# The first batch's values of an agent-attention kernel, loaded as 112 and 8 rows in place of 128

## The chip, the cores and the metric

One core of one Trainium2 chip runs the whole program. The metric is the device time of one execution, in microseconds; the kernel before is given by the median of three runs.

## What is computed

Two layers follow each other. The attention has 49 agents per batch between queries and keys (B = 2 batches, N = 12480 tokens, C = 128 channels), the second layer is a leaky-ReLU MLP of width 2048 without biases:

```
a2k     = softmax(scale * agents @ k^T)      # 49 x N, per batch
agent_v = a2k @ v                            # 49 x C, per batch
q2a     = softmax(scale * q @ agents^T)      # N x 49
x       = q2a @ agent_v                      # N x C
h       = x @ w_in;  g = max(0.01 * h, h);  out = g @ w_out
```

## The kernel before

The host lays the values out as `v[b, p, j, c]`, 120 rows `p` of 104 columns `j` of 130 floats (128 channels, a one for the denominator, a zero). A chunk `c` is eight columns, so that a row of a chunk is 8 * 130 * 4 = 4160 contiguous bytes, and a batch has 13 chunks. Keys are laid out as `k[b, :, j, :]` with 128 channels as rows of 8 * 120 * 4 = 3840 bytes, again 13 chunks.

The work has two stages. In the first, some 53 us long, the first batch's attention is done while everything it needs is streamed in: the 13 chunks of keys, the weights as eight transfers of 512 KB (64-bit words, taken apart by `conv_bits`, line 262, and its companions), two blocks of queries, then the 13 chunks of values. All loads are issued by SyncE (SP) in the order of the string `ORDER` (line 134): `"kwqwkkkqwkkkwkkkkkkwvvwvvvvvvvvvwvvwq"`. In the second stage a loop over 52 blocks of 480 tokens runs `mm1`, `relu_hi`, `relu_lo` and `mm2` in eight steps a block, with the queries' chain, and in the first 26 blocks the second batch's attention, put into its side steps.

The order of the first stage's instructions on each engine is worked out at build time by `Plan` (line 19) from costs written by hand: each load is a step on "sp" and one on "dma", each consumer a step on its engine. A values' chunk is a step of 1280 on "dma" (line 1124). The order is then fixed; on the chip an engine waits where its operand isn't there yet. `heat` (line 1106) are products of zeros that the plan puts into TensorE's gaps.

`load_v` (line 217) loads one chunk of values into a tile of a ring of nine (`ld`, shared with the keys). For the first batch it transfers 128 rows, of which the last eight are the first rows of the second batch, and nobody reads them. For the second batch it transfers the 120 rows alone (line 224). SP issues each transfer when its tile is free and when an earlier transfer's completion counter is free again.

The consumer in the first stage is `k_av32` (line 561): for each column a product of the exponentials of the scores, `s_sb`, with `v_t[b, c][:TP, j, :]`, rows 0 to 119, sixteen matmul records per chunk (each fp32 product shows as two), 208 in all, summed in one PSUM tile `av`. The chunks are taken in the order in which they are loaded. When the last is in, the chain `f_copy` (574), `f_tr`, `f_den`, `f_rec`, `f_avT`, `m_half` (666), `m_hi_of`, `m_lo_of` ends in the first `mm1` (869).

For the last two transfers of weights, `conv_bits` (273, 274) waits on VectorE for the weights to land; `conv_low` (289), `conv_sign` (296) and `conv_mul` (303) come behind it. `ww_tr` (316) and `ww_mm` (330) are products of the weights on TensorE. `p_move` and `p_dup` (856, 860) are SP's transfers from SBUF to SBUF of 64 and 32 rows.

Of the kernel before, what the change touches and what calls it, by code (L numbers as in the profile page):

```python
# [74 lines left out]
def tile_agent_attention_then_leaky_mlp(  # L75
# [27 lines left out]
    nc = tc.nc  # L103
# [3 lines left out]
    P = 128  # L107
    TP = 120
# [108 lines left out]
    def load_v(b, c):  # L217

        t = ld.tile([P, CH, C + 2], F32, tag="ld", name="vt")
        j = slice(c * CH, (c + 1) * CH)  # L220
        if b == 0:
            nc.sync.dma_start(out=t, in_=v.rearrange("b p j c -> (b p) j c")[:P, j, :])
        else:
            nc.sync.dma_start(out=t[:TP], in_=v[b, :, j, :])
        v_t[b, c] = t
# [811 lines left out]
    for b in range(1, B):  # L1037
# [21 lines left out]
        for h in range(NH):  # L1059
            s = n0 + h * NP // 2  # L1060
            if h % 2 == 0:
                c = h // 2
                at(s - 5, load_v, b, c)
                at(s, k_sub, b, c, nc.gpsimd)
                at(s + 2, k_exp, b, c)
            at(s + 3, k_ehi, b, h, h, nc.scalar)
            at(s + 3, k_elo, b, h, h, nc.gpsimd)
            at(s + 1, k_vhi, b, h, h, nc.vector)
            at(s + 2, k_vlo, b, h, h, nc.gpsimd)
            if h % 2:  # L1070
                at(s + lag, k_av2, b, h // 2)
# [10 lines left out]
    with tc.manual_schedule():  # L1082
# [10 lines left out]
        for o, a, n in SLOTS:  # L1093
            nc.gpsimd.tensor_tensor(
                out=sel[:, o:o + n], in0=ident[:EW, a:a + n],
# [3 lines left out]
            out=less, in0=ident[:EW, :NA + 1], in1=ident[:EW, HALF:EW + 1], op=ALU.add  # L1099
# [6 lines left out]
        def heat(n, start=False):  # L1106
# [15 lines left out]
        fetch = {  # L1122
            "k": (lambda c: load_k(0, c), 1210),
            "v": (lambda n: load_v(0, TURN[n]), 1280),
            "w": (load_w, 1250), "q": (load_q, 610),
        }
# [30 lines left out]
        for n in range(w7):  # L1157
            r = [("mul", n - RP)] if n >= RP else []
# [166 lines left out]
```

## Time and profile before

| what | us |
|---|---|
| median of three runs | 951.16 (951.0 to 951.84) |
| the profiled execution, its own time | 951.56 |
| the profiled execution, its span | 949.5 |
| TensorE busy | 942.2 (99% of the span) |
| VectorE busy | 738.7 (78%) |
| ScalarE busy | 615.0 (65%) |

The span runs from the profile's first instruction to its last; about 2 us of the execution's own time lie around it. TensorE is busy nearly throughout, but a busy share is an average: in the first stage TensorE waits for other engines and for transfers, and the profile counts some of that waiting as matmuls that are still in the pipeline.

### The profile page before, as it was taken

How to read it: one execution, taken by the hardware profiler on the slowest of the kernel's cores; microseconds unless marked ns; L12 is line 12 of the kernel's file. 1: busy time of each engine (PE TensorE's matmuls, PEld its weight loads, DVE VectorE, ACT ScalarE, POOL GpSimd, SP SyncE). 2: the span in 40 equal slices, each digit the busy share in tenths (PEclk: the TensorE clock that was granted, in tenths of full speed). 3: DMA queues.
4: the chain of work that ended last, by engine and by line, in shares of the span. 5: the costliest groups of instructions: out<-in, count | busy, mean ns of one | idle time of the engine just before them, and what ended most of it. 6: DMA issues, size and time to landing. Idle time of an engine off the chain costs nothing.

```text
span 949.5 us, 22897 instructions
## 1 busy us (share of the span) xinstructions
PE 942.2 (99%) x9422; PEld 892.6 (94%) x9422; DVE 738.7 (78%) x1070; ACT 615.0 (65%) x912; POOL 382.1 (40%) x563
## 2 busy tenths in 40 slices
PE   9999999999999999999999999999999999999998
PEld 8878898889999999999999999999999999998998
DVE  7987777687888888888887777777777777777775
ACT  5675665666666666666677666666666666666654
POOL 1003432334565665665554433343433433343420
PEclk9999999999999999999999999999999999999999
DMA  9932224113223123231121121212111121112110
GB/s 345 408 95 75 75 85 129 61 43 87 62 63 96 54 73 86 57 84 51 43 51 35 43 53 43 53 43 53 32 48 48 43 54 43 52 43 54 32 42 22
DMA packets 28867, 70.25 MB, mean 74 GB/s; under 512 B 4419, under 2 KB 17859, under 8 KB 28763
## 3 DMA queue, kind: packets, MB, share of 16 engines
q1 hardware_dynamic: 28763, 68.79, 23.9%
q8 instruction: 74, 1.21, 0.5%
q14 instruction: 30, 0.25, 0.1%
HBM read 43.22 MB, written 12.78 MB: 59 GB/s over the span
## 4 chain that ended last, share of the span: by engine, by line
PE 95%; DVE 2%; DMA 2%; issue 0%; SPq 0%; ACT 0%; DVEq 0%; ACTq 0%
PE turn L913 58%; PE h L876 28%; PE turn L741 2%; DMA kt<-in_k_dram 2%; PE turn L924 2%; PE turn L390 1%; PE turn L535 1%; PE sc L390 1%; DVE s_sb L495 0%; PE turn L638 0%; PE turn L333 0%; PE av L567 0%; PE turn L320 0%; PE turn L947 0%; PE e L947 0%
## 5 line engine op out<-in xcount | busy, mean ns | idle before, releaser
L893 DVE SCALAR_TENSOR_TENSOR lo<-h,hi 128x960 fp32r<-128x960 f32 x416 | 478.7, 1151 | 183.9 <-ACT hi L887 183.6
L887 ACT ACTIVATE hi<-h 128x960 fp32r<-128x960 f32 x416 | 405.8, 976 | 288.6 <-PE h L876 276.7
L913 PE MATMUL turn<-hi,wo_hi 64*128 64x480 f32 x1656 | 402.5, 379 | 0.0
L913 PE MATMUL turn<-hi,wo_lo 64*128 64x480 f32 x1656 | 399.8, 376 | 0.0
L876 PE MATMUL h<-pT,m_hi 64*128 64x480 f32 x1664 | 319.7, 377 | 0.1
L913 PE MATMUL turn<-lo,wo_hi 64*128 64x480 f32 x1656 | 317.5, 375 | 0.0
L913 PEld LDWEIGHTS turn<-hi,wo_lo 64*128 64x128 f32 x1656 | 252.3, 184 | 7.5
L913 PEld LDWEIGHTS turn<-hi,wo_hi 64*128 64x128 f32 x1656 | 248.9, 184 | 7.1
L876 PEld LDWEIGHTS h<-pT,m_hi 64*128 64x128 f32 x1664 | 222.8, 184 | 9.7 <-DVE lo L893 0.9
L913 PEld LDWEIGHTS turn<-lo,wo_hi 64*128 64x128 f32 x1656 | 223.7, 184 | 8.3
L876 PE MATMUL h<-pT,m_lo 64*128 64x480 f32 x832 | 226.0, 376 | 0.1
L876 PEld LDWEIGHTS h<-pT,m_lo 64*128 64x128 f32 x832 | 131.1, 184 | 5.1 <-DVE m_lo L697 0.8
L355 POOL TENSOR_TENSOR qlo<-qt,qhi 128x480 fp32r<-128x480 f32 x50 | 61.3, 1225 | 70.0 <-ACT qhi L712 70.0
L355 POOL TENSOR_TENSOR pT<-pt,pT 64x480 fp32r<-64x480 f32 x50 | 60.9, 1218 | 59.3 <-ACT pT L841 59.3
L784 POOL COPY mx<-mx 32x15 f32<-32x15 f32 x50 | 9.4, 188 | 181.7 <-DVE mx L777 181.7
L355 POOL TENSOR_TENSOR d<-st,mm 64x375 f32<-64x375 f32 x50 | 41.3, 827 | 89.3 <-DVE mm L790 84.1
L972 POOL TENSOR_TENSOR oT<-oT 128x480 f32<-128x480 f32 x51 | 62.4, 1224 | 12.7 <-issue 10.0
L967 ACT COPY oT<-turn 128x480 f32<-128x480 f32 x102 | 51.9, 561 | 0.9 <-PE turn L913 0.9
L827 POOL TENSOR_TENSOR pd<-d,rs 64x375 f32<-64x375 f32 x50 | 40.9, 817 | 28.8 <-DVE rs L822 28.2
L784 POOL COPY sm<-sm 32x15 f32<-32x15 f32 x50 | 9.4, 188 | 96.1 <-DVE sm L807 93.7
L741 PE MATMUL turn<-qhi,a_hl 64*128 64x240 f32 x208 | 43.6, 274 | 0.0
L741 PE MATMUL turn<-qlo,a_hl 64*128 64x240 f32 x208 | 43.3, 271 | 0.0
(195 smaller groups left out, 928.6 us busy)
## 6 DMA issues: line engine op xcount, KB each, us to landing
kt<-in_k_dram SPq DMA_DIRECT2D x26, 480.0 KB, 5.7
qt<-in_q_dram SPq DMA_DIRECT2D x52, 240.0 KB, 2.9
pT<-pT SPq DMA_DIRECT2D x102, 120.0 KB, 2.3
out_dram<-oT SPq DMA_DIRECT2D x51, 240.0 KB, 2.0
vt<-in_v_dram SPq DMA_DIRECT2D x13, 520.0 KB, 10.0
vt<-in_v_dram SPq DMA_DIRECT2D x13, 487.5 KB, 4.5
w<-in_w_in_dram SPq DMA_DIRECT2D x4, 512.0 KB, 8.4
w<-in_w_out_dram SPq DMA_DIRECT2D x4, 512.0 KB, 9.6
```

The source lines that it names most:

```text
L355: eng.tensor_tensor(out=o, in0=x, in1=y, op=ALU.subtract)
L390: nc.tensor.matmul(ps[r, j * w:j * w + NA], lhsT=k_t[b, c][:, j, r], rhs=a_sb[:, b, :], start=j == 0 or not late(b, c), stop=True, skip_gr ...
L741: nc.tensor.matmul(s_t[i][:, m, :h], lhsT=a_hl[i // BPB][r], rhs=x[r, m * h:(m + 1) * h], start=(s == 0 and n == 0), stop=(n == 1), skip_g ...
L784: by(i).tensor_copy(r[x, :, 1], r[y, :, 0])
L827: by(i).tensor_tensor(out=pd[:n, :, :A0], in0=d[:n], in1=w[:n].to_broadcast([n, NT, A0]), op=ALU.mult,)
L876: nc.tensor.matmul(ps[:, g, :NB], lhsT=w[b][r, cols(2 * p + g)], rhs=t[r, x], start=(n == 0), stop=(n == 2),)
L887: nc.scalar.activation(hi, h_t[i, p][:, :, :NB], AF.Relu)
L893: nc.vector.scalar_tensor_tensor(out=lo, in0=h_t.pop((i, p))[:, :, :NB], scalar=0.0, in1=hi.bitcast(F32), op0=ALU.max, op1=ALU.subtract,)
L913: nc.tensor.matmul(o[g][:, :NB], lhsT=w[r], rhs=x[r], start=start, stop=stop)
L924: nc.tensor.matmul(o[g][:, :NB], lhsT=w[b][r], rhs=t[r, x], start=False, stop=False)
L967: nc.scalar.copy(t[:, g], o[g][:, :NB])
L972: nc.gpsimd.tensor_tensor(out=t[:, 0], in0=t[:, 0], in1=t[:, 1], op=ALU.add)
```

## The change

The first batch's values: each chunk is loaded by two transfers, rows 0 to 111 and rows 112 to 119, both from the first batch, in place of one transfer of 128 rows of which eight belong to the second batch.

```diff
         j = slice(c * CH, (c + 1) * CH)
         if b == 0:
-            nc.sync.dma_start(out=t, in_=v.rearrange("b p j c -> (b p) j c")[:P, j, :])
+            for r in (slice(0, TP - 8), slice(TP - 8, TP)):
+                nc.sync.dma_start(out=t[r], in_=v[0, r, j, :])
         else:
             nc.sync.dma_start(out=t[:TP], in_=v[b, :, j, :])
```

Nothing else differs: the plan's costs, the order of the loads and the consumers are the same.

## Rows read from the trace of the kernel before

**Rows 1.** The page: the span, and the DMA engines' busy tenths in 40 slices.

```profile
span 949.5 us, 22897 instructions
...
DMA  9932224113223123231121121212111121112110
```

**Rows 2.** Windows of the first stage: stretch, length, engines' busy time, clock, DMA share, GB/s.

```profile
core 0: us, PE busy (x) PEld busy (x) DVE busy (x) ACT busy (x) POOL busy (x), PEclk, DMA share, GB/s
26.00:28.00 2.00, 0.57 (x17) 0.44 (x13) 1.46 (x3) 0.63 (x1) 0.00 (x0) 1.00 1.00 401
30.00:44.00 14.00, 13.45 (x192) 12.34 (x190) 13.34 (x39) 10.07 (x20) 0.00 (x0) 1.00 1.02 411
```

**Rows 3.** SP's timeline: start, time, what; in merged rows with SP's waits between the issues.

```profile
24.24 14.48 SPq L222 DMA_DIRECT2D vt<-in_v_dram  x9
38.82 0.38 SPq L240 DMA_DIRECT2D w<-in_w_in_dram  x1
39.29 1.57 SPq L222 DMA_DIRECT2D vt<-in_v_dram  x2
40.96 0.38 SPq L245 DMA_DIRECT2D w<-in_w_out_dram  x1
```

**Rows 4.** Transfers issued from 20 to 45 us: count, KB each, median us to landing.

```profile
vt<-in_v_dram SPq DMA_DIRECT2D x13, 520.0 KB, 10.0
w<-in_w_out_dram SPq DMA_DIRECT2D x2, 512.0 KB, 9.6
w<-in_w_in_dram SPq DMA_DIRECT2D x1, 512.0 KB, 7.5
```

**Rows 5.** The transfers issued from 40 to 40.9 us: the last chunk of values.

```profile
vt<-in_v_dram SPq DMA_DIRECT2D x1, 520.0 KB, 8.8
```

**Rows 6.** TensorE's timeline: the products with the values, chunks 0 to 8 and 11 to 12.

```profile
36.38 8.19 PE L567 MATMUL av<-vt,s_sb 120*49 120x130 f32 x144
...
48.13 2.04 PE L567 MATMUL av<-vt,s_sb 120*49 120x130 f32 x32
```

**Rows 7.** The chain that ended last, in order of time, around the last values.

```profile
47.55 0.66 PE turn L320 x4
48.20 1.97 PE av L567 x32
...
50.24 0.68 PE turn L333 x4
```

**Rows 8.** Windows inside loads of 120 rows, second batch: the first, one between, the last.

```profile
219.40:220.80 1.40, 1.40 (x17) 1.26 (x16) 0.91 (x3) 0.97 (x1) 0.38 (x2) 1.00 0.87 273
...
341.00:342.40 1.40, 1.40 (x17) 1.40 (x15) 0.98 (x1) 0.42 (x2) 0.34 (x1) 1.00 0.91 253
...
427.40:428.80 1.40, 1.40 (x17) 1.40 (x15) 0.62 (x3) 0.97 (x1) 0.89 (x3) 1.00 1.01 289
```

**Rows 9.** A window in the second stage in which transfers of 128 rows run (keys).

```profile
146.00:148.00 2.00, 2.00 (x22) 1.72 (x20) 0.61 (x2) 0.94 (x2) 0.12 (x1) 1.00 0.96 355
```

**Rows 10.** A window in which two SBUF-to-SBUF transfers of 32 rows run.

```profile
199.00:200.30 1.30, 1.30 (x35) 1.15 (x36) 1.08 (x3) 0.98 (x2) 0.00 (x0) 1.00 0.88 186
```

**Rows 11.** The values' instructions by line: SP's issues, ns min/median/max, first and last start.

```profile
L222 SPq DMA_DIRECT2D vt<-in_v_dram x13: 328/328/693, 20.7 to 40.2; - x13
```

**Rows 12.** VectorE's timeline after the last values were issued.

```profile
47.41 0.42 DVE L273 TENSOR_SCALAR em<-w 128x512 int32<-128x512 int32 x1
...
49.40 0.69 DVE L303 TENSOR_TENSOR w_out_sb<-w_out_sb,e 128x512 f32<-128x512 f32 x1
50.01 0.69 DVE L289 SCALAR_TENSOR_TENSOR w_in_sb<-w,w_in_sb 128x512 f32<-128x512 uint32 x1
51.59 0.16 DVE L600 TENSOR_SCALAR den<-den 128x1 f32<-128x1 f32 x1 [0.89 <-PE den L586]
...
51.86 0.42 DVE L273 TENSOR_SCALAR pre<-w 128x512 int32<-128x512 int32 x1
```

**Rows 13.** The page's DMA issues: the second batch's values, KB each, median us to landing.

```profile
vt<-in_v_dram SPq DMA_DIRECT2D x13, 487.5 KB, 4.5
```

## The prediction

> **What bounds the kernel now.** I read the page first: the span is 949.5 us, and of the 40 slices of the DMA engines only the first two, 0 to 47 us, stand at nine tenths [rows 1]. So the change touches a stage in which the DMA engines are full. The windows show how full: from 30 to 44 us, when the values arrive, the 16 DMA engines are busy with a share of 1.02 and move 411 GB/s [rows 2]. A chunk of values, 128 * 4160 = 532,480 bytes, thus takes 532,480 / 411 = 1.296 us.
>
> Then I asked whether anything waits for them. SP runs well ahead: it issues the values in a long row from 24.24 us on [rows 3], and a chunk lands 10.0 us after its issue [rows 4], so some eight chunks are under way at a time. The last two chunks are issued from 39.29 to 40.86 us, the last one at about 40.2 us, and it lands 8.8 us later, at 49.0 us [rows 3, 5]. TensorE takes chunks 0 to 8 in one stretch from 36.38 us without a gap and the last two from 48.13 us on in 2.04 us, so that the last one is begun at about 49.15 us [rows 6]. The chain that ended last runs from VectorE into a transposition of weights on TensorE at 47.55 us, and from there straight into these products [rows 7]. The values are therefore not on the path, but 49.15 - 49.0 = 0.15 us beside it. If they land earlier, TensorE still comes from VectorE's work at 47.55 us: nothing to gain. If they land later by more than 0.15 us, everything behind moves by the rest.
>
> **The change, part by part.**
>
> *Removed: eight unread rows a chunk.* 13 * 8 * 4160 = 432,640 bytes; at 411 GB/s they are 1.05 us of the DMA engines' time over the whole stage. As shown, at most nothing of that reaches the end.
>
> *The 112 rows.* No first-batch transfer of fewer than 128 rows is in the trace, but the second batch's values are loaded with rows of the same 4160 bytes and 120 rows. In windows put inside these 13 loads the DMA share is 0.87 to 1.01, yet they move only 253 to 289 GB/s, 267 in the mean of the 13 [rows 8]. Keys of 128 rows move at 355 GB/s with a share of 0.96 in the same second stage, beside the same engines' work [rows 9], and the first stage's transfers of 128 rows run at 411. So busy engines move a third less when a transfer doesn't cover the 128 partitions, and this is not a matter of idle engines. Transfers of 32 rows, from SBUF to SBUF, are slower yet: 186 GB/s at a share of 0.88 [rows 10]. The bounds are 411 GB/s (the split costs nothing) and 186 GB/s. 112 rows are nearest to 120, so I take 267: 112 * 4160 = 465,920 bytes in 1.745 us.
>
> *The eight rows.* 33,280 bytes. The nearest row is the one with the fewest partitions, 32 [rows 10]: at 186 GB/s 0.18 us. A chunk then costs 1.745 + 0.18 = 1.92 us, 0.63 us more than now. The ends for a whole chunk of 499,200 bytes: at 411 GB/s 1.215 us (0.08 us less), at 186 GB/s 2.68 us (1.39 us more).
>
> [...]
>
> *Sum on the path.* All 13 chunks stand ahead of the last landing: 13 * 0.63 = 8.2 us later, 57.2 us in place of 49.0. Less the 0.15 us of slack, plus the second completion that the first product of the last chunk now waits for: one more wait, bounded by 0 and 0.2 us, taken at 0.15. What stands behind the last product, from 50.24 us on [rows 7], moves by 8.2 us.
>
> *SP.* 13 more issues of 0.33 to 0.69 us [rows 11], 4.3 to 9 us, on a queue that has some eight chunks' time ahead of the landing. Behind them stand two transfers of weights and one of queries. With two transfers a chunk the same number under way is four chunks, some 7.7 us of work at the new pace, so the DMA engines do not run dry. Cost nothing; if that cover were gone, it is a rival below.
>
> *What else is late.* The seventh transfer of weights now lands at 38.82 + 7.5 = 46.3 us [rows 3, 4]; eleven of the chunks are ahead of it, so it moves by 11 * 0.63 = 6.9 us to 53.2 us. VectorE needs it for the bits at 47.41 us and then stands still for 5.8 us; behind that wait are 3.3 us of work up to the end of line 289 at 50.7 us, now 56.5 us [rows 12]. The next instruction, line 600, waits for TensorE's denominator, which moves from 51.59 to 59.8 us: 3.3 us to spare. The product at 50.24 us needs line 303 of 49.40 us, now done at 55.9 us, before 58.4 us. The eighth transfer lands at 40.96 + 9.6 = 50.6 us now and at 58.8 us then; it is needed at 51.86 + 8.2 = 60.1 us. The queries and the SBUF transfer of block 1 are needed some steps after the first product with queries and move with it. None adds to the sum.
>
> **Forecast.** 951.56 + 8.2 = 959.8 us for the profiled execution; the median of the runs shown is 0.4 us below that execution, so 959.4 us. The likeliest case's own range takes 0.4 us a chunk (rather better packing than for 120 rows) to 1.0 us a chunk (halfway to the rate of the 32 rows): 5.2 and 13 us, 956.4 to 964.2 us.
>
> **The rivals.**
>
> *Not slower: the rows cost no more than now.* If each DMA engine is the limit by itself, and not where it writes, no engine has more bytes than before, and the stream ends where it ended, or up to 1.05 us earlier; with nothing to gain at 47.55 us the time is 951.2 us. It decides as soon as the last chunk lands before 49.15 us. For it: a share of 1.02 in the stage [rows 2] reads as engines at their own limit. Against it: the 120-row loads have nearly the same share and two thirds of the rate [rows 8]. [...] Chance 0.17.
>
> *SP's limit on transfers under way.* If the count under way is eight transfers, and a round trip is longer than four chunks at the old pace, 5.2 us, the engines run dry once a chunk. A lone 120-row load lands after 4.5 us [rows 13], which is shorter; at 5.7 us the price would be (5.7 - 5.2) / 4 * 13 = 1.6 us, 952.6 us. Chance 0.03.
>
> *TensorE's clock falls on top.* [...] Chance 0.07.
>
> *The transfer on the path after all.* If the profile's chain hides a wait for the values in those products, the 1.05 us saved would count: 950.1 us. Even this is within 0.2%. Chance 0.03, and what remains of it is all that speaks for a real gain.
>
> **How the numbers follow.** The forecast keeps 0.70. A measurement of this kernel can tell about 0.2% from no change, 1.9 us: the forecast and the clock rival are slower (0.77), with a little for the upper half of SP's rival (0.01); the others are within it, 0.20, and 0.02 stays for faster. The range has to take in the not-slower rival to hold 8 in 10: 950.8 to 965 us.
>
> **What would show it.** In the profile after, the DMA share from 30 us on stays near 1 while the rate falls from 411 to about 260 GB/s, and the full slices end some 8 us later. The values' products no longer form one stretch of 144 from 36.38 us but come chunk by chunk, about 1.9 us apart, with the chain through DMA on the values; the last ends near 58 us in place of 50.17. VectorE waits at line 273 for weights for 5 to 6 us. From the first block on the two traces run alike, shifted. The prediction is wrong if the rate stays at 400 GB/s or more, or if the products end by 51 us; it is wrong in size if a chunk costs under 0.4 or over 1.0 us more.

## The result, and the profile after

The changed kernel takes 964.22 us (median of four executions, 962.86 to 966.1), the kernel before 951.08 us in the same comparison: a ratio of 1.0138, with an interval of 1.012 to 1.0157. It is slower by 13.1 us. The forecast was 959.4 us, with 950.8 to 965 as its range: the direction and the place were right, the price was too low.

The profile shown is that of the execution of 966.1 us. First its page: the span, TensorE's granted clock and the DMA engines' busy tenths, in 40 slices.

```profile
span 964.1 us, 22911 instructions
...
PEclk9979999999999999999999999999999999999999
DMA  9980242221231322322112111111212121212110
```

The span is 14.6 us longer than before [rows 1]. The full DMA slices now reach into the third one, and in that third slice (48 to 72 us) the clock stands at seven tenths; in the page before every slice stands at nine:

```profile
PEclk9999999999999999999999999999999999999999
```

The windows of the first stage:

```profile
core 0: us, PE busy (x) PEld busy (x) DVE busy (x) ACT busy (x) POOL busy (x), PEclk, DMA share, GB/s
30.00:44.00 14.00, 10.53 (x139) 8.94 (x137) 10.48 (x30) 7.80 (x16) 0.00 (x0) 1.00 1.02 245
54.00:56.00 2.00, 2.00 (x16) 1.41 (x13) 0.00 (x0) 0.00 (x0) 0.00 (x0) 0.50 1.05 237
64.00:66.00 2.00, 2.00 (x12) 1.73 (x9) 0.00 (x0) 0.30 (x2) 0.00 (x0) 0.50 0.03 10
```

From 30 to 44 us the DMA share is 1.02, as before, and the rate 245 GB/s in place of 411 [rows 2]. This is the change in one row: the DMA engines are as busy and move 40% less. The share counts the time that packets took. By these two rows a row of 4160 bytes occupied an engine for some 0.17 us before (16 * 1.02 * 4160 bytes / 411 GB/s, an estimate) and for 0.28 us now. The chain that ended last, in order of time:

```profile
36.25 8.94 DMA vt<-in_v_dram
...
45.21 0.02 SPq L223
...
45.25 7.41 DMA vt<-in_v_dram
...
52.68 9.60 DMA vt<-in_v_dram
...
62.37 1.98 PE av L568 x16
...
67.33 0.48 ACT m_hi L694
...
67.85 1.03 PE h L877 x6
```

Before, the chain came through VectorE and a transposition into the last products with the values [rows 7]. Now it goes from landing to landing. Between them the chain passes through SP (line 223), whose next issue waits for an earlier transfer's completion: eight such waits for values, 9.0 us in all and 1.6 us the longest, from 15 to 70 us. That alone does not make SP the limit: the DMA share stays at 1.02, and the first experiment tests it. The last issue of values, the eight rows of the last chunk, lands at 52.68 + 9.60 = 62.28 us, 13.3 us after the 49.0 us of before. TensorE's timeline shows what that does to the products with the values (line 567 is line 568 now):

```profile
38.20 2.87 PE L568 MATMUL av<-vt,s_sb 120*49 120x130 f32 x48
...
46.91 1.09 PE L568 MATMUL av<-vt,s_sb 120*49 120x130 f32 x16 [0.53 <-DMA vt<-in_v_dram]
48.77 1.09 PE L568 MATMUL av<-vt,s_sb 120*49 120x130 f32 x16 [0.77 <-DMA vt<-in_v_dram]
50.90 1.10 PE L568 MATMUL av<-vt,s_sb 120*49 120x130 f32 x16 [1.03 <-DMA vt<-in_v_dram]
```

One stretch of 144 [rows 6] has broken up into single chunks. The last three shown start 1.9 and 2.1 us apart, each behind an idle time that ended when values landed. Behind the last chunk stands a second loss. From its begin to the first product with queries the trace of before takes 53.05 - 49.15 = 3.9 us; here it is 67.85 - 62.37 = 5.5 us, because those products run at a granted clock of 0.50 (the sixteen of the last chunk take 1.98 us, where a chunk at 1.00 takes 1.09). So 13.3 us come from the landing and 1.5 us from the clock in this execution; in the rest of the span the two kernels are level within 0.2 us.

VectorE's timeline shows the predicted wait for the weights behind the values, and the slack behind it:

```profile
57.67 0.43 DVE L274 TENSOR_SCALAR em<-w 128x512 int32<-128x512 int32 x1 [7.32 <-DMA w<-in_w_in_dram]
...
66.18 0.16 DVE L601 TENSOR_SCALAR den<-den 128x1 f32<-128x1 f32 x1 [5.22 <-PE den L587]
```

VectorE waits 7.3 us for weights and then still 5.2 us for TensorE's denominator: the weights are late, and are not what ends last.

The transfers of weights tell what the forecast left out. The first of these three rows is a transfer ahead of all values in the kernel before (issued at 19.4 us), the second the same transfer in the changed kernel (issued at 19.2 us), the third the transfer behind the eleventh chunk there, issued at 48.7 us (KB each, us to landing):

```profile
w<-in_w_in_dram SPq DMA_DIRECT2D x1, 512.0 KB, 9.7
```

```profile
w<-in_w_in_dram SPq DMA_DIRECT2D x1, 512.0 KB, 12.8
...
w<-in_w_in_dram SPq DMA_DIRECT2D x1, 512.0 KB, 8.9
```

A transfer of 128 rows that is itself unchanged, and stands ahead of the values in the queue, lands 3.1 us later after its issue. It is still under way, until 32.0 us, when the rate falls:

```profile
26.00:28.00 2.00, 0.55 (x16) 0.42 (x13) 1.16 (x2) 0.63 (x1) 0.00 (x0) 1.00 1.06 357
28.00:30.00 2.00, 1.56 (x57) 1.47 (x53) 1.13 (x2) 0.00 (x0) 0.00 (x0) 1.00 1.04 216
```

That engines which are done with it early begin the values' rows and get in the way of the others is the author's guess: no run shows single engines.

### The profile page after: what moved, and what is told of

It is laid out like the page before. It is cut to its first block, busy times and chain, and to the rows that moved or that the text cites. A ratio compares the mean times of both kernels' runs of the same rounds, so it can differ in the third digit from the quotient of the medians.

```text
span 964.1 us, 22911 instructions
## 1 busy us (share of the span) xinstructions
PE 947.4 (98%) x9422; PEld 892.1 (93%) x9422; DVE 738.7 (77%) x1070; ACT 614.6 (64%) x912; POOL 382.2 (40%) x563
## 4 chain that ended last, share of the span: by engine, by line
PE 93%; DMA 6%; DVE 1%; SPq 0%; ACT 0%; issue 0%; ACTq 0%
PE turn L914 57%; PE h L877 28%; DMA vt<-in_v_dram 3%; PE turn L742 2%; PE turn L925 2%; PE turn L391 1%; DMA w<-in_w_in_dram 1%; PE turn L536 1%; DMA kt<-in_k_dram 1%; DMA w<-in_w_out_dram 1%; PE turn L334 0%; PE turn L639 0%; PE av L568 0%; PE turn L948 0%; PE e L948 0%; PE turn L677 0%
## 5 line engine op out<-in xcount | busy, mean ns | idle before, releaser
L914 PE MATMUL turn<-hi,wo_hi 64*128 64x480 f32 x1656 | 398.2, 379 | 0.0
L914 PE MATMUL turn<-hi,wo_lo 64*128 64x480 f32 x1656 | 395.5, 376 | 0.0
L877 PE MATMUL h<-pT,m_hi 64*128 64x480 f32 x1664 | 313.9, 377 | 0.1
L914 PE MATMUL turn<-lo,wo_hi 64*128 64x480 f32 x1656 | 311.7, 375 | 0.0
L877 PEld LDWEIGHTS h<-pT,m_hi 64*128 64x128 f32 x1664 | 218.3, 184 | 10.5 <-DVE lo L894 1.1
L914 PEld LDWEIGHTS turn<-lo,wo_hi 64*128 64x128 f32 x1656 | 219.2, 184 | 9.1
L877 PE MATMUL h<-pT,m_lo 64*128 64x480 f32 x832 | 221.7, 376 | 0.2 <-DVE m_lo L698 0.2
L828 POOL TENSOR_TENSOR pd<-d,rs 64x375 f32<-64x375 f32 x50 | 40.9, 818 | 28.8 <-DVE rs L823 28.2
```

The lines of the kernel that those rows point to most:

```text
L828: by(i).tensor_tensor(out=pd[:n, :, :A0], in0=d[:n], in1=w[:n].to_broadcast([n, NT, A0]), op=ALU.mult,)
L877: nc.tensor.matmul(ps[:, g, :NB], lhsT=w[b][r, cols(2 * p + g)], rhs=t[r, x], start=(n == 0), stop=(n == 2),)
L914: nc.tensor.matmul(o[g][:, :NB], lhsT=w[r], rhs=x[r], start=start, stop=stop)
```

## The experiments

Two theories were set against each other. **Theory A**: the DMA engines meet at the places they write, because a transfer of fewer than 128 rows does not lay them side by side. **Theory B**: the number of transfers costs, by an overhead of each or by the limit on how many are under way. That engines meet is the author's picture, and no trace shows it, nor how many rows of a transfer an engine takes; what the runs can show is the rate by the partitions that are written. Within A it was open whether the 112 rows (A1) or the eight rows (A2) cost it.

**As many transfers, split by columns.**

```diff
-            nc.sync.dma_start(out=t, in_=v.rearrange("b p j c -> (b p) j c")[:P, j, :])
+            vv = v.rearrange("b p j c -> (b p) j c")
+            for g in range(2):
+                u = slice(g * G, (g + 1) * G)
+                nc.sync.dma_start(
+                    out=t[:, u, :], in_=vv[:P, c * CH + g * G:c * CH + (g + 1) * G, :]
+                )
```

> Each chunk as two transfers again, 26 in all, but split by columns: 128 rows of four columns (2080 bytes) each. Theory A (what costs is that the transfer does not cover the 128 partitions, so that engines meet at the places they write): rate from 30 to 44 us stays near 400 GB/s, at most some 5% lower for the shorter rows, time 951 to 953 us. Theory B (what costs is the number of transfers: their overhead, or the limit on how many are under way): as the changed kernel, rate near 245 GB/s and 960 to 966 us.

Measured: 951.33 us, ratio 0.9999 (0.9989 to 1.0008). Its window from 30 to 44 us:

```profile
30.00:44.00 14.00, 13.45 (x207) 12.33 (x203) 12.99 (x38) 9.31 (x19) 0.00 (x0) 1.00 1.04 384
```

26 transfers cost nothing that can be measured. The rate of 384 GB/s is 7% below the 411 of before, a little more than expected, and far from 245. Theory B falls.

**One transfer of 120 rows.**

```diff
-            nc.sync.dma_start(out=t, in_=v.rearrange("b p j c -> (b p) j c")[:P, j, :])
+            nc.sync.dma_start(out=t[:TP], in_=v[0, :, j, :])
```

> Each chunk as one transfer of 120 rows, 13 in all, as the second batch does it. Theory A: the rate falls to 250 to 290 GB/s from 30 to 44 us, a chunk costs 0.5 to 0.75 us more, and the weights behind are slowed too; time 958 to 965 us. Theory B: the number of transfers is that of the kernel before, so 951 to 952 us.

Measured: 966.21 us, ratio 1.0149 (1.0134 to 1.0164), a little over what theory A expected, with as many transfers as the kernel before.

```profile
30.00:44.00 14.00, 11.04 (x148) 9.30 (x146) 11.34 (x33) 8.13 (x16) 0.00 (x0) 1.00 0.97 255
```

This is the rate of the second batch's loads [rows 8], now in a stage in which something waits for it. So the 128-row transfer with its eight unread rows does work: it is worth some 15 us here.

**The 112 rows alone.** The last eight rows of each chunk are neither loaded nor summed.

```diff
-            nc.sync.dma_start(out=t, in_=v.rearrange("b p j c -> (b p) j c")[:P, j, :])
+            nc.sync.dma_start(out=t[:TP - 8], in_=v[0, :TP - 8, j, :])
...
-                av_t[b][o:o + NA], lhsT=s_sb[:, c, j, :], rhs=v_t[b, c][:TP, j, :],
+                av_t[b][o:o + NA], lhsT=s_sb[:TP - 8, c, j, :], rhs=v_t[b, c][:TP - 8, j, :],
```

> The 112 rows alone, 13 transfers; the last eight rows of each chunk are neither loaded nor summed (the contraction is over 112 rows). [...] Theory A2 (the eight rows cost it: they fall on few places): rate near 400 GB/s, 951 to 952 us. Theory B: 951 to 952 us.

Measured: 962.38 us, ratio 1.0111 (1.0095 to 1.0128).

```profile
30.00:44.00 14.00, 10.54 (x122) 8.69 (x118) 12.06 (x35) 9.26 (x18) 0.00 (x0) 1.00 1.04 242
```

11.0 of the 13.1 us are there without the eight rows, at 242 GB/s where A2 expected near 400: A1.

**The eight rows beside a whole transfer.** They go into a tile that nobody reads (its own lines are left out here), at partitions 8c to 8c + 7, so at another place for each chunk.

```diff
             nc.sync.dma_start(out=t, in_=v.rearrange("b p j c -> (b p) j c")[:P, j, :])
+            r, u = slice(8 * c, 8 * c + 8), slice(c * CH, c * CH + 7)
+            nc.sync.dma_start(out=spare[r], in_=v[0, TP - 8:, u, :])
```

> The 128-row transfer as in the kernel before, and beside each one transfer of eight rows (seven columns of them, 3640 bytes) that nobody reads, into a tile of its own; 26 transfers. [...] Theory A2: 0.5 us or more a chunk, 957 to 961 us. Theory B: 960 to 966 us.

Measured: 954.96 us, ratio 1.0034 (1.0021 to 1.0047), below what A2 and B expected: 3.55 / 13 = 0.27 us a chunk, for seven eighths of the bytes. The changed kernel over the 112 rows alone gives 13.1 - 11.0 = 2.1 us, 0.17 us a chunk, loosely, since the intervals of the two ratios overlap. The eight rows thus cost more than their bytes, which are 0.07 us at 411 GB/s, and less than a third of what the change costs. What they cost beside a whole transfer when they always go to partitions 112 to 119, as in the change, was not tried.

**Places.** The next two kernels load 64 rows a chunk with one transfer and sum partitions 32 to 63 alone; the other rows are left out. They differ in which 64 rows are taken, and so in the partitions that are written: 32 to 95, or 0 to 63 (the second has `slice(0, 64)`). Each was run once, and what is read from it is the rate: if the number of rows alone matters, it is the same in both, and if the partitions do, it need not be.

```diff
-            nc.sync.dma_start(out=t, in_=v.rearrange("b p j c -> (b p) j c")[:P, j, :])
+            r = slice(32, 96)
+            nc.sync.dma_start(out=t[r], in_=v[0, r, j, :])
...
-                av_t[b][o:o + NA], lhsT=s_sb[:, c, j, :], rhs=v_t[b, c][:TP, j, :],
+                av_t[b][o:o + NA], lhsT=s_sb[32:HALF, c, j, :], rhs=v_t[b, c][32:HALF, j, :],
```

> One transfer of 64 rows a chunk, partitions 32 to 95; only partitions 32 to 63 are summed. [...] Theory A without places (any transfer of fewer than 128 rows is slow): 200 to 270 GB/s. [...]

Partitions 32 to 95, two windows of it (from 28 us the values, with a transfer of weights under way among them; later TensorE's clock):

```profile
28.00:33.00 5.00, 4.33 (x66) 3.62 (x61) 3.87 (x8) 2.69 (x5) 0.00 (x0) 1.00 1.03 408
...
50.00:62.00 12.00, 12.00 (x82) 10.00 (x79) 1.08 (x5) 2.36 (x5) 0.00 (x0) 0.50 0.43 128
```

> The same with partitions 0 to 63, the same 64 rows' length, engines, counts and sums of partitions 32 to 63. [...] Without places: the same rate as for partitions 32 to 95. Time near 951 us.

Partitions 0 to 63:

```profile
28.00:33.00 5.00, 3.96 (x61) 3.25 (x57) 3.08 (x7) 1.30 (x3) 0.00 (x0) 1.00 1.04 222
...
43.00:50.00 7.00, 7.00 (x62) 6.44 (x58) 5.66 (x11) 6.19 (x10) 0.00 (x0) 0.50 1.02 220
```

The same bytes, rows, engines' share and number of transfers: 408 GB/s at partitions 32 to 95, 222 at 0 to 63. In windows of 2 us from 28 to 34 us it is 412, 407 and 372 against 215, 230 and 228. So it is not the number of rows; it goes with the partitions. The pair alone doesn't part the rows that are read from the places they are written to, and rows 32 to 95 were not loaded into partitions 0 to 63; the two halves below, which read the very rows of the kernel before, speak for the places. How the rows of a transfer are spread over the engines no trace here shows. Both times, 961.28 and 962.29 us, missed the 951 us that was expected; the second rows show where the time went, and the last section says what is known of it.

**Two halves of 64 rows.** All 128 rows, in two transfers of partitions 0 to 63 and 64 to 127 (`ROWS`); 64 rows divide by the 16 engines as evenly as 128. The rival of theory A here is that division.

```diff
-            nc.sync.dma_start(out=t, in_=v.rearrange("b p j c -> (b p) j c")[:P, j, :])
+            vv = v.rearrange("b p j c -> (b p) j c")
+            for r in ROWS:
+                nc.sync.dma_start(out=t[r], in_=vv[r, j, :])
```

> [...] Rival (the uneven load of the engines in the changed kernel is what costs: 112 and 120 rows do not divide evenly): 951 to 952 us.

Measured: 966.47 us, ratio 1.0145 (1.0124 to 1.0166).

```profile
30.00:44.00 14.00, 9.31 (x100) 7.52 (x98) 10.95 (x33) 8.46 (x17) 0.00 (x0) 1.00 1.03 240
```

Nothing was dropped and nothing divides unevenly, and it costs 15 us at 240 GB/s: the price needs no uneven division. The split by columns read the same rows with as many transfers and cost nothing (951.33 us). Apart from the shorter rows that the columns give, the two differ only in which partitions one transfer covers.

**Three transfers, the middle one well placed.** `SL` is 32.

```diff
-            nc.sync.dma_start(out=t, in_=v.rearrange("b p j c -> (b p) j c")[:P, j, :])
+            vv = v.rearrange("b p j c -> (b p) j c")
+            for r in (slice(SL, 3 * SL), slice(0, SL), slice(3 * SL, P)):
+                nc.sync.dma_start(out=t[r], in_=vv[r, j, :])
```

> 128 rows a chunk as three transfers: partitions 32 to 95, then 0 to 31, then 96 to 127; 39 transfers. [...] If only the number of rows per transfer or the number of transfers mattered: 966 us or more.

Measured: 961.15 us, ratio 1.0106 (1.0087 to 1.0125), 5.3 us below the two halves with 13 transfers more.

```profile
30.00:44.00 14.00, 10.95 (x129) 9.18 (x128) 12.27 (x36) 9.26 (x18) 0.00 (x0) 1.00 0.92 254
44.00:52.00 8.00, 4.99 (x74) 3.95 (x71) 4.46 (x9) 5.39 (x8) 0.00 (x0) 1.00 1.01 274
```

So neither the number of transfers nor the rows of each settle the time alone. At 254 to 274 GB/s a chunk of 532,480 bytes takes 1.9 to 2.1 us, at the 240 GB/s of the halves 2.2. Not all of the gain is transfers: between the two profiles the begin of the last chunk's products moves from 63.85 to 58.07 us, by 5.8 us, and another 1.0 us lies behind it (5.0 and 4.0 us to the first product with queries), where the clock fell in the halves (0.54 from 64 to 66 us) and not here (1.00 from 52 to 68 us).

**The clock.** Products of zeros on TensorE in the waits of the changed kernel, put there to keep the granted clock at 1.00, first many, then, beside the changed kernel, fewer (the lines of `heat` itself are left out).

```diff
+        if g == 1 and 2 <= n < NCH - 1:
+            heat({10: 10, 11: 6}.get(n, 4))
```

> The changed kernel with four products of zeros on TensorE behind each of the values' chunks 2 to 9, ten behind chunk 10 and six behind chunk 11, in the waits for the next chunk. [...]

Measured: 965.95 us, ratio 1.0154 (1.0138 to 1.0169). In its profile the granted clock is 1.00 from 50 to 68 us, as it was meant to be, but TensorE goes without an idle time from the products of zeros (62.22 us, 1.60 us long) into the last chunk's at 63.76 us, so they may have delayed it.

> The changed kernel once more, beside the next one on the same chip: 963 to 966 us.

Measured: 963.58 us (961.44 to 965.86), ratio 1.0128 (1.0107 to 1.0149).

> The changed kernel with fewer products of zeros in its waits than before (three behind chunks 2 to 9, eight behind chunk 10, five behind chunk 11), so that they end before the next chunk lands. [...]

Measured: 964.43 us (963.6 to 966.38), ratio 1.0142 (1.0125 to 1.0159). No gain in either. The timeline of this last kernel, from the last chunk to the first product with queries, and the chain of the changed kernel's second profile, in which the clock stayed at 1.00 without any help:

```profile
61.04 1.09 PE L576 MATMUL av<-vt,s_sb 120*49 120x130 f32 x16
...
65.02 0.71 PE L887 MATMUL h<-pT,m_hi 64*128 64x480 f32 x4
```

```profile
51.48 8.69 DMA vt<-in_v_dram
...
60.27 1.11 PE av L568 x16
...
64.24 1.02 PE h L877 x4
```

Behind the last chunk both take 4.0 us at a clock of 1.00, where the first profile took 5.5 at 0.50 (until 66 us): where the clock falls it costs the 1.5 us, and where it stays they are saved. But the last chunk lands at another time in each execution, at 62.28 us in one profile of the changed kernel and at 60.17 us in the other, and that hides it. What the clock is worth in the median stays open.

## Why the prediction was right, and where it was too low

*What bounds the stage.* Right. The values stood 0.15 us beside the path, and a later landing moved everything behind it one to one: in the changed kernel's second profile the last chunk lands 60.17 - 49.0 = 11.2 us later, and its span is 960.6 us, 11.1 us longer.

*The rate.* Right in kind: the 120-row loads of the second batch were the row to take, and the 120-row kernel showed the same rate in the first stage. Its reading, that a transfer which "doesn't cover the 128 partitions" is slow, was too wide: 64 rows at partitions 32 to 95 moved at 408 GB/s, and two halves that together cover all 128 at 240. The forecast's chunk of 1.92 us is 260 GB/s; measured were 245 and, in the second profile, these two windows:

```profile
44.00:52.00 8.00, 4.91 (x68) 3.91 (x70) 5.70 (x11) 6.24 (x10) 0.00 (x0) 1.00 1.00 251
52.00:60.00 8.00, 4.17 (x54) 3.17 (x53) 3.26 (x6) 1.72 (x3) 0.00 (x0) 1.00 1.03 251
```

*The term that was mis-sized.* "All 13 chunks stand ahead of the last landing: 13 * 0.63 = 8.2 us later" counted the chunks alone. At 251 GB/s a chunk of 499,200 bytes takes 1.99 us, 0.69 more than now, and 13 of them 9.0 us. Two transfers of weights stand between the chunks, in windows of the same 251 GB/s, though transfers of 128 rows moved at 411 before: 524,288 bytes at 251 in place of 411 GB/s are 0.81 us more each, 1.6 us. That makes 10.6 of the 11.2 us. The rest belongs to transfers that were issued ahead of the values. These are the kernel before and the second profile of the changed one, from 27 us, where the rate begins to fall, to the last landing:

```profile
27.00:48.94 21.94, 20.29 (x316) 18.13 (x318) 19.83 (x50) 14.91 (x27) 0.00 (x0) 1.00 1.00 398
```

```profile
27.00:60.17 33.17, 21.97 (x318) 18.12 (x318) 22.00 (x53) 16.64 (x30) 0.00 (x0) 1.00 1.02 252
```

252 GB/s over 33.17 us are 8.4 MB, and the chunks with the two weights are 7.5 of them. Some 0.8 MB of earlier transfers were thus still to come and went at the low rate, 1.3 us more by the same reckoning. The sum of 11.9 us is then a little over the 11.2, since the kernel before holds 398 GB/s in this stretch and not 411. The price belongs to the stretch in which such transfers are under way, and not to their own bytes.

*The range.* The likeliest case's own range ended at 964.2 us, with 1.0 us a chunk; a chunk cost 0.69 us more in the second profile, well inside, and the time came out at that edge by terms that the sum had at nothing. That the stated range, up to 965 us, still holds the 964.22 us is in part luck.

*The eight rows.* Taken at 0.18 us; 0.17 us by the difference of two kernels, which is loose, and 0.27 us beside a whole transfer. By the reckoning above, the gap to the 964.22 us measured is filled by the weights and the transfers ahead of the values, and by the clock.

*SP and the second wait.* Right: with 26 transfers of 128 rows each the time is that of before (951.33 us, ratio 0.9999), so neither 13 more issues, nor four chunks under way in place of eight, nor the second wait cost anything that can be measured. The 0.15 us at which the second wait was taken is shown by no run.

*What else is late.* Right in what waits: VectorE stood still for weights, 7.3 us where 5.8 were forecast, and then had 5.2 us to spare where 3.3 were.

*The rivals.* "Not slower" fell: a share of 1.02 reads like engines at their own limit and is not one, as 222 GB/s at a share of 1.04 shows. That no engine has more bytes than before was its assumption, which no run shows; the halves, which move the very bytes of before, cost 15 us. "TensorE's clock falls on top" happened in most executions: the mean granted clock was 0.995 to 0.998 in seven of the changed kernel's eight. It cost 1.5 us in the first of the two that were profiled, and nothing in the second, where it stayed at 1.00. The change does what it says, and what it saves, 1.05 us of transfers, is not seen.

No version beats the kernel before: the values are off its path, so the best that another split could do is to equal it, as the split by columns does.

## What to carry to other kernels

In this first stage a transfer's price went with the partitions that it writes: 128 rows moved at 411 GB/s and 64 rows at partitions 32 to 95 at 408, but 64 rows at 0 to 63 at 222, 112 rows at 242 and 120 rows at 255. Read rate and share together: here a full DMA share with a low rate (1.02 with 245 GB/s) went with the partitions that were written, and dropping the unread rows to save bytes was a loss of 13.1 us. Count such a transfer's price on everything that is under way beside it, a transfer ahead of it too: the weights ahead of the values landed after 12.8 us in place of 9.7.

## What the runs showed of the hardware that was not expected

TensorE's granted clock fell although TensorE was busy. In the two kernels of 64 rows the products with the values run over 32 partitions in place of 120; TensorE shows 12.00 us busy in 12.00 from 50 to 62 us, with a granted clock of 0.50 (partitions 32 to 95; 0.50 from 43 to 50 us with partitions 0 to 63), and the times, 961.28 and 962.29 us, are 10 us and more over the 951 us that was expected. In the first of the two these products begin at 35.80 us, and the clock falls while they run:

```profile
36.00:38.00 2.00, 2.00 (x40) 2.00 (x38) 1.89 (x7) 1.69 (x5) 0.00 (x0) 1.00 0.03 8
38.00:40.00 2.00, 2.00 (x28) 1.98 (x26) 1.90 (x8) 1.62 (x4) 0.00 (x0) 0.65 0.84 223
```

It is back at 1.00 from 64 us on (windows up to 70 us). From the first of these products to the first product with queries it takes 27.0 us (to 62.79 us), before 16.7 us (36.38 to 53.05 us), which is where the 10 us lie. With 120 partitions the clock stayed at 1.00 in the same stage of the kernel before. What the two kernels share apart from the fewer partitions, the rows left out, was not tried alone, so what makes the clock fall stays open.

A transfer of 64 rows at partitions 32 to 95 reached the rate of 128 rows, 408 against 411 GB/s.
